# An attention norm with one activation in place of two, and the last tile's rows stored in six transfers in place of twelve

## The chip, the core and the metric

One Trainium2 chip, one of its cores. The metric is the device time of one execution in microseconds (us). The kernel before was timed three times: 264.51, 264.31 and 264.94 us, median 264.51. One more execution was taken with the hardware profiler; it took 264.59 us, and its span from the first to the last instruction is 262.6 us.

## The reference

Eight batches, eight heads, 576 positions, head size 64. Per head a 64 x 64 product of k and v, then q times it, then a norm over the 64 elements of each row; the heads are laid side by side into a token matrix of 4608 x 512, which goes through a two-layer network with a quick GELU.

```python
kv  = einsum('bhsd,bhse->bhde', k, v)
out = einsum('bhsd,bhde->bhse', q, kv)
rms = sqrt(mean(out * out, axis=-1) + 1e-6)
x   = (out / rms * g_norm) laid out as (4608, 512)
h   = x @ w_in                      # 512 -> 2048
g   = h * sigmoid(1.702 * h)
out = g @ w_out                     # 2048 -> 512, float32
```

## The kernel before

**Tiles.** The 4608 tokens are worked through in nine tiles of 512. Tile t (0 to 7) holds the first 512 positions of batch t. The 64 positions that each batch has left over are gathered in `x_rem` and make tile 8, which the code calls `t == B`. Batches 0 and 1 (`EARLY`) take their positions in another order, so that their left-over rows lie six rows apart in the output, where those of the other batches lie one below the other.

**Order.** The order of the instructions on each engine is the order in which the program issues them (`manual_schedule`). While the projections of tile t run on TensorE, the attention of batch t + 1 is slipped between them: `at1` and `at2` (lines 953 to 957) attach such units to the number of a matmul group, and the tables `FIRST`, `LATER` and `LAST_TWO` (lines 906 to 938) hold the numbers. Tiles 2 to 8 do their two matrix products by seven block products in place of eight (classes `SevenIn` and `Seven`).

**The norm.** There are two forms of it. Where the head elements lie along the partitions (batches 0 and 1, and the left-over 64 rows of every batch), `out` (line 260) makes the product, ScalarE squares it (line 272), a matmul with a block matrix of ones adds the squares up (`sums`, line 335), ScalarE takes the logarithm of the mean plus 1e-6 (line 337) and then `rs` (line 343) the exponential of minus half of that; VectorE multiplies (`apply`, lines 348 to 359). Where the rows lie along the partitions (the 512 rows of batches 2 to 7), VectorE adds the squares up (`add_up`), `roots` does the logarithm and the exponential on 128 x 16 elements, two times per batch (lines 310 and 311), and `turn` multiplies and has SP transpose the result by DMA. Logarithm and exponential come from one activation table set, the GELU from another; `preload_act_table_set` (lines 173, 331, 1005, 1019) loads them.

For batch 0 `sums` and `rs` are placed apart by hand (lines 857 to 871), with work for other heads in between; everywhere else `ss` calls one right after the other.

**The last tile's stores.** Tile 8 has 512 rows in four row blocks `mo` of 128 rows; block `mo` holds the left-over rows of batches 2 mo and 2 mo + 1, 64 partitions each. `Seven.run` (line 648) takes the block products of tile 8 in the order `LAST`; after the sums of a quarter `place` (line 629) puts them into `osb` on VectorE and calls `store_rest` (line 681): after the second quarter for blocks 0 and 1 with all 512 columns, then for block 2 and block 3 with the upper 256 columns, then for block 2 and block 3 with the lower 256. `store_rest` issues one transfer per batch: the first on SP's queue, the second on ScalarE's:

```python
for g in range(2):
    rows = out[(2 * mo + g) * S : (2 * mo + g + 1) * S, n0:n1]
    ...
    queue = (nc.sync, nc.scalar)[g]
    queue.dma_start(out=rows, in_=osb[g * R : (g + 1) * R, mo, n0:n1])
```

On the side of SBUF such a transfer counts 64 partitions, and on the side of DRAM 64 rows. The only other transfer on ScalarE's queue is that of `g_row` (line 136), 64 float32 in a single row.

Of the kernel before, what the change touches and what calls it, by code (L numbers as in the profile page):

```python
# [8 lines left out]
F32 = mybir.dt.float32  # L9
ALU = mybir.AluOpType  # L10
AFT = mybir.ActivationFunctionType

P = 128
# [3 lines left out]
def kernel(  # L17
# [10 lines left out]
    nc = tc.nc  # L28

    B, H, S, D = q.shape  # L30
    DM = H * D
# [5 lines left out]
    SM = 512  # L37
    J = SM // P
    R = S - SM
    assert R == 64 and B * R == SM and KO == NPAIR and 2 * D == P  # L40
    NT = B + 1
    EARLY = 2
    PE_ = 96
    NJ = S // PE_
# [5 lines left out]
    attn = ctx.enter_context(tc.tile_pool(name="attn", bufs=4))  # L50
# [20 lines left out]
    eps_t = const.tile([P, 1], F32)  # L71
# [4 lines left out]
    HF, HN = FO // 2, DM // 2  # L76
# [51 lines left out]
    for n in "kqv":  # L128
        if n != "q":
            rows = stage.tile([P, 6, 2 * P], F32, name="qf", tag="qf", bufs=2)  # L130
            rows = rows.rearrange("p h x -> p (h x)")[0:PE_]
# [8 lines left out]
        out=ident,  # L140
        in_=ident,
# [28 lines left out]
    load_w_in(10, 13)  # L170
    load_w_in(13, FO)

    nc.scalar.preload_act_table_set("natural_log_exp_and_others")
    nc.vector.memset(eps_t, EPS)
    one_t = const.tile([1, 1], F32)
    nc.vector.memset(one_t, 1.0)
# [18 lines left out]
    class Attention:  # L195
# [76 lines left out]
            nc.scalar.activation(sq[:, 0:n], t, AFT.Square)  # L272
            self.o[c] = (t, sq, n)

        def ss(self, c, table=False):
            self.sums(c, table)
            self.rs(c)


        def rows(self, i):  # L280

            pool, tag = (ps_h, "hT") if i < 3 else (ps_a, "att")
# [24 lines left out]

        def roots(self, h):
            s4 = self.sum4[:, 2 * h : 2 * h + 2, :]
            nc.scalar.activation(s4, s4, AFT.Ln, bias=eps_t, scale=1.0 / D)  # L310
            nc.scalar.activation(s4, s4, AFT.Exp, bias=0.0, scale=-0.5)

        def turn(self, j):
            j0, c0 = j // 2 * 2, j % 2 * (DM // 2)
# [11 lines left out]
                    in_=self.x16[:, j - 1 : j + 1, :].rearrange("p j n -> p (j n)"),  # L326
                )

        def sums(self, c, table=False):
            if table:  # L330
                nc.scalar.preload_act_table_set("natural_log_exp_and_others")
            o, sq, n = self.o[c]
            pool, tag = self.ss_pool
            t = pool.tile([P, SM], F32, name="ss", tag=tag)
            nc.tensor.matmul(t[:, 0:n], ones2, sq[:, 0:n], start=True, stop=True)  # L335
            ln = attn.tile([P, SM], F32, name="ln", tag="ln", bufs=2)
            nc.scalar.activation(ln[:, 0:n], t[:, 0:n], AFT.Ln, bias=eps_t, scale=1.0 / D)  # L337
            self.o[c] = (o, ln, n)

        def rs(self, c):  # L340
            o, ln, n = self.o[c]
            rs = attn.tile([P, SM], F32, name="rs", tag="rs", bufs=2)
            nc.scalar.activation(rs[:, 0:n], ln[:, 0:n], AFT.Exp, bias=0.0, scale=-0.5)
            self.o[c] = (o, rs, n)

        def apply(self, c):
# [142 lines left out]
    def copy(engine, to, src):  # L489
        (nc.vector.tensor_copy if engine == "D" else nc.scalar.copy)(to, src)  # L490
# [77 lines left out]
    class Seven:  # L568
# [60 lines left out]
        def place(self, name, mo, with_, i, j):  # L629
            ps, m = self.ready(name, mo)  # L630
            if ps is None:
                return
            o = osbs[self.t][:, 2 * i + m.start : 2 * i + m.stop, j * HN : (j + 1) * HN]
            if with_:
                nc.vector.tensor_add(o, ps, self.kept[with_][:, m])  # L635
            else:
                copy = nc.vector.tensor_copy if self.t == B else nc.scalar.copy
                copy(o, ps)  # L638
            if self.t == B:
                if (i, j) == (0, 1):  # L640
                    store_rest(0, 0, DM)
                    store_rest(1, 0, DM)
                elif i == 1:
                    store_rest(2 + mo, j * HN, (j + 1) * HN)
            elif self.t in HALVED and j == 1 - i:
                store(self.t, 2 * i, 2 * i + 2)

# [30 lines left out]
                            u()  # L678
                        n += 1

    def store_rest(mo, n0, n1):
        osb = osbs[B]
        for g in range(2):
            rows = out[(2 * mo + g) * S : (2 * mo + g + 1) * S, n0:n1]
            if 2 * mo + g < EARLY:
                p0 = SM % PE_
                rows = rows[bass.DynSlice(NJ * p0 + SM // PE_, R, step=NJ), :]
            else:
                rows = rows[SM:S, :]
            queue = (nc.sync, nc.scalar)[g]  # L690
            queue.dma_start(out=rows, in_=osb[g * R : (g + 1) * R, mo, n0:n1])

    def hid_seven(t, hid, seven, units1):

# [118 lines left out]
    def store(t, j0, j1):  # L813
        nc.sync.dma_start(
            out=out[t * S : t * S + SM, :].rearrange("(p j) m -> p j m", j=J)[:, j0:j1],
            in_=osbs[t][:, j0:j1],
        )


    a0 = First(0)  # L820
# [33 lines left out]
    a0.out(0)  # L854
    a0.q(1)
    a0.kv(1)
    a0.sums(0)
    a0.out(1)
    a0.q(2)
    a0.rs(0)  # L860
    a0.kv(2)
    a0.sums(1)
    a0.apply(0)
    a0.out(2)
    a0.rs(1)
    a0.q(3)
    a0.apply(1)
    d0 = Hidden(0)
    d0.mm(0, 0)
    a0.sums(2)  # L870
    a0.rs(2)
    d0.mm(0, 1)
    d0.mm(0, 2)
    d0.mm(0, 3, ps_a, "att")
# [29 lines left out]
    osbs = {}  # L904
# [35 lines left out]
    def plan(t):  # L940
        return LATER if t < B - 1 else LAST_TWO
# [7 lines left out]
    for t in range(NT):  # L949
        b = t + 1  # L950
        u1, u2 = {}, {}

        def at1(i, f, *args):
            u1.setdefault(i, []).append(lambda: f(*args))

        def at2(i, f, *args):
            u2.setdefault(i, []).append(lambda: f(*args))  # L957

        def of(b, name, *args):
            return lambda: getattr(live[b], name)(*args)  # L960

        if t == 0:
            at1(7, of(0, "out", NPAIR))
            at2(4, setattr, a0, "ss_pool", Attention.ss_pool)
            at2(4, of(0, "ss", NPAIR, True))
            at2(4, of(0, "apply", NPAIR))
            at1(8, start, 1)
            at2(5, scale_w_in, 0, nc.scalar)
            at2(6, scale_w_in, 1, nc.scalar)
            at2(33, weight_sum, 0)  # L970
            at2(33, scale_w_in, 2, nc.vector)
            at2(34, scale_w_in, 3, nc.vector)
            for n, at in ((2, 35), (0, 39), (1, 40)):
                at2(at, w_in_sum, n)
            for l in range(2):
                at1(9, nc.vector.memset, kvd[l], 0.0)
            at1(13, load_q, 2)
            for c in range(NPAIR):
                at1(12, of(1, "pack_q", c))
                at2(9 + 3 * c, of(1, "q", c))  # L980
                at2((36, 37, 46, 47)[c], of(1, "kv", c))
                o = (41, 43, 52, 53)[c]
                at2(o, of(1, "out", c))
                if c == NPAIR - 1:
                    at2(48, load_kv, 2)
                at2((45, 48, 56, 58)[c], of(1, "ss", c))
                at2((48, 51, 56, 60)[c], of(1, "apply", c))
        elif b < B:
            if t == 1:
                for n in range(1, 4):  # L990
                    at1(0, weight_sum, n)
                at1(9, w_in_sum, 3)
            todo = plan(t) if t >= SEVEN else None
            at1(todo.steps.index("kv") if todo else 11, of(b, "kv_all", todo.keep if todo else "D"))
            late = 15 if todo else 11
            if t == 1:
                at1(5, start, b)
                at1(5, of(b, "transpose_q"))
            if t + 2 < B:
                at1(late, load_kv, t + 2)  # L1000
                at1(late, load_q, t + 2)
                at2(100, start, t + 2)
                at2(100, of(t + 2, "transpose_q"))
            at = todo.attn if todo else FIRST
            at2(at["table"], nc.scalar.preload_act_table_set, "natural_log_exp_and_others")
            for h in range(2):
                at2(at["roots"][h], of(b, "roots", h))
            for j in range(J):
                for name in ("rows", "add_up", "turn"):
                    at2(at[name][j], of(b, name, j))  # L1010
            at2(46, of(b, "out", NPAIR))
            at2(74, of(b, "ss", NPAIR))
            at2(80, of(b, "apply", NPAIR))
            at2(82, nc.scalar.preload_act_table_set, "gelu_apprx_sigmoid_and_others")
        elif t < B:
            for name in ("ss_pool", "rest_pool"):
                at2(16, setattr, live[1], name, (ps_a, "att"))
            at2(16, of(1, "out", NPAIR))
            at2(34, nc.scalar.preload_act_table_set, "natural_log_exp_and_others")
            at2(44, of(1, "ss", NPAIR))  # L1020
            at2(50, of(1, "apply", NPAIR))
            at2(52, nc.scalar.preload_act_table_set, "gelu_apprx_sigmoid_and_others")
        dense(t, u1, u2, (GROUP, 5)[t] if t < 2 else 0, t == 0, None if t else d0)
# [30 lines left out]
```

## Time and profile before

| | |
|---|---|
| time, median of 3 | 264.51 us (264.31 to 264.94) |
| profiled execution | 264.59 us |
| its span, first to last instruction | 262.6 us |
| mean granted TensorE clock | 0.997 |
| TensorE matmul busy | 254.4 us, 97% of the span |
| VectorE busy | 185.6 us, 71% |
| ScalarE busy | 183.5 us, 70% |
| moved by DMA | 35.32 MB |

Times in the views count from the start of the span. PE is TensorE's matmuls, PEld its weight loads, DVE is VectorE, ACT is ScalarE, POOL is GpSimd, SP is SyncE; SPq and ACTq are the instructions with which SP and ScalarE issue transfers. A group of instructions reads: line, engine, operation, output<-input, shapes, count, then busy us, mean ns of one, idle us before them and what ended the idle time. A row of the busy view by stretches reads: the stretch and its length, the busy us (and count) of PE, PEld, DVE, ACT and POOL, the granted clock in that stretch, the busy share of the core's 16 DMA engines and the GB/s that they moved. A row of a DMA queue reads: packets, MB, and the time that the packets took as a share of 16 engines over the stretch asked for. q10 is ScalarE's DMA queue, q1 is SP's. The line on DMA packets counts those under 512 B, under 2 KB and under 8 KB, each number holding the one before it.

### The profile page before, as it was taken

To read this page: it belongs to the slowest core of one execution; us is meant where nothing else is said; L and a number is where in the kernel's file an instruction comes from. 1 tells how busy PE (TensorE), PEld (TensorE's weight loads), DVE (VectorE), ACT (ScalarE), POOL (GpSimd) and SP (SyncE) were. 2 spreads that over 40 slices of the span, in tenths; PEclk is the share of its full clock that TensorE was granted. 3 is DMA by queue.
4 is the path that set the end of the run, shared out by engine and by line. 5 is a ranking of instruction groups with operands and counts; after the bars stand their busy time and mean duration, and the time that the engine had idled before them with its cause. 6 is when DMAs were issued, how large, how long until landed. Compare 5 with 4: busy or idle time off the path is not lost.

```text
span 262.6 us, 6224 instructions
## 1 busy us (share of the span) xinstructions
PE 254.4 (97%) x2556; PEld 204.6 (78%) x2556; DVE 185.6 (71%) x324; ACT 183.5 (70%) x336; POOL 42.7 (16%) x66
## 2 busy tenths in 40 slices
PE   7789999999999999999999999999999999999993
PEld 6334444446988988899889988998899888888882
DVE  2540287768758995899589958995899677557841
ACT  3569856886648974897479847984699469837810
POOL 8864242005005000500050005000000000000000
PEclk9999999999999999999999999999999999999998
DMA  7999999998999946996799769946800620012005
GB/s 178 177 199 205 204 203 182 200 228 113 175 158 169 230 59 163 115 239 81 159 150 197 88 164 149 236 52 160 165 11 2 159 83 0 2 80 82 0 2 160
DMA packets 59870, 35.32 MB, mean 135 GB/s; under 512 B 31554, under 2 KB 57154, under 8 KB 59714
## 3 DMA queue, kind: packets, MB, share of 16 engines
q0 software_dynamic: 28512, 17.91, 49.7%
q1 hardware_dynamic: 30848, 16.49, 27.9%
q10 hardware_dynamic: 482, 0.52, 0.6%
q8 instruction: 20, 0.33, 0.5%
q14 instruction: 8, 0.07, 0.1%
HBM read 36.70 MB, written 9.44 MB: 176 GB/s over the span
## 4 chain that ended last, share of the span: by engine, by line
PE 93%; POOL 3%; DMA 3%; DVE 0%; issue 0%
PE o L658 37%; PE h L540 33%; PE hT L432 10%; PE o L770 5%; DMA vbuf<-in_v_dram 3%; PE kvp L221 2%; PE outR L286 2%; POOL qraw L89 1%; PE ss L335 1%; POOL kraw L89 1%; PE outT L254 0%; POOL vbuf L89 0%; PE q L413 0%; PE outT L258 0%; POOL w_in_sb L153 0%; DVE osb L638 0%
## 5 line engine op out<-in xcount | busy, mean ns | idle before, releaser
L658 PEld LDWEIGHTS <-gS 128*128 128x128 f16 x512 | 49.8, 98 | 5.6
L520 ACT ACTIVATE gT<-h 128x512 f16<-128x512 f32 x84 | 46.2, 605 | 5.2 <-PE h L540 5.2
L540 PEld LDWEIGHTS <-ws 128*128 128x128 f16 x448 | 43.8, 98 | 5.1
L658 PE MATMUL o<-tw,gS 128*128 128x256 f16 x384 | 46.3, 273 | 0.0
L540 PE MATMUL h<-xS,ws 128*128 128x256 f16 x336 | 45.3, 273 | 0.0
L658 PEld LDWEIGHTS <-gT 128*128 128x128 f16 x384 | 37.1, 98 | 4.2
L540 PEld LDWEIGHTS <-w_in_sb 128*128 128x128 f16 x336 | 32.5, 98 | 3.9
L658 PE MATMUL o<-w_out_sb,gT 128*128 128x256 f16 x256 | 33.3, 273 | 0.0
L432 PE MATMUL hT<-xT,w_in_sb 128*128 128x512 f16 x128 | 28.9, 379 | 0.7 <-DMA w_in_sb<-in_moe_w_in_dram 0.7
L540 PE MATMUL h<-xT,w_in_sb 128*128 128x256 f16 x192 | 27.1, 273 | 0.0
L635 DVE TENSOR_TENSOR osb<-o,qf 128x512 f32<-128x512 f32 (+1 forms) x25 | 16.7, 668 | 13.7 <-PE o L658 10.9
L89 POOL DMA_DIRECT2D kraw<-in_k_dram x11 | 8.0, 731 | 106.5 <-PE kvp L221 88.4
L554 DVE TENSOR_TENSOR h<-h,s 128x512 f32<-128x512 f32 x28 | 19.6, 698 | 7.4 <-PE h L540 5.6
L590 DVE TENSOR_TENSOR gS<-gT 128x512 f16<-128x512 f16 (+2 forms) x34 | 22.0, 653 | 3.9 <-ACT gT L441 3.2
L432 PEld LDWEIGHTS <-w_in_sb 128*128 128x128 f16 x128 | 12.3, 98 | 15.7 <-DMA w_in_sb<-in_moe_w_in_dram 1.3
L556 DVE TENSOR_TENSOR s<-h,s 128x512 f32<-128x512 f32 x28 | 19.4, 692 | 3.9 <-PE h L540 3.3
L441 ACT ACTIVATE gT<-hT 128x512 f16<-128x512 f32 x32 | 17.6, 613 | 5.4 <-PE hT L432 5.3
L337 ACT ACTIVATE ln<-ss,eps_t 128x512 f32<-128x512 f32 (+1 forms) x16 | 9.3, 581 | 14.0 <-PE ss L335 13.9
L520 ACT ACTIVATE gT<-s 128x512 f16<-128x512 f32 x28 | 17.3, 628 | 1.2 <-DVE s L556 1.2
L957 ACT ACT_TABLE_LOAD x14 | 18.0, 1283 | 0.2
L770 PE MATMUL o<-w_out_sb,gT 128*128 128x512 f16 x64 | 16.7, 380 | 0.0
L490 ACT COPY s<-h 128x512 f32<-128x512 f32 x17 | 10.0, 588 | 9.5 <-PE h L540 8.8
(94 smaller groups left out, 369.4 us busy)
## 6 DMA issues: line engine op xcount, KB each, us to landing
out_dram<-osb SPq DMA_DIRECT2D x10, 512.0 KB, 4.2
kraw<-in_k_dram POOLq DMA_DIRECT2D x6, 576.0 KB, 8.7
vbuf<-in_v_dram POOLq DMA_DIRECT2D x6, 576.0 KB, 12.2
qraw<-in_q_dram POOLq DMA_DIRECT2D x3, 512.0 KB, 13.2
qbuf<-in_q_dram POOLq DMA_DIRECT2D x3, 512.0 KB, 14.3
out_dram<-osb SPq DMA_DIRECT2D x6, 192.0 KB, 6.6
w_in_sb<-in_moe_w_in_dram POOLq DMA_DIRECT2D x4, 256.0 KB, 8.0
w_out_sb<-in_moe_w_out_dram POOLq DMA_DIRECT2D x2, 512.0 KB, 13.8
```

The lines of the kernel that those rows point to most:

```text
L89: nc.gpsimd.dma_start(out=raw[n][0:PE_, c0:c1, :].rearrange("p c (l x) -> p (c l) x", l=2), in_=early_src(n, b, c0, c1),)
L432: nc.tensor.matmul(self.h[fo], w_in_sb[:, ko, fo * P : (fo + 1) * P], self.x[:, ko], start=(ko == 0), stop=(ko == KO - 1),)
L441: nc.scalar.activation(self.gT[:, fo, :], self.h[fo], AFT.Gelu_apprx_sigmoid)
L520: nc.scalar.activation(self.gT[:, to, n * TH : (n + 1) * TH], src, AFT.Gelu_apprx_sigmoid)
L540: nc.tensor.matmul(bank[name][:, a], w, x, start=(p in (1, 5) and a == 0 and k == 0), stop=(k == KH - 1), skip_group_check=True,)
L554: nc.vector.tensor_add(bank["z"], bank["x"], self.s5)
L556: nc.vector.tensor_add(self.s5, bank["x"], self.s5)
L590: op(s[:, n, lo], a, b)
L635: nc.vector.tensor_add(o, ps, self.kept[with_][:, m])
L658: nc.tensor.matmul(o, a, w, start=(p in (1, 2, 5) and i == 0 and (mo == 0 or split)), stop=(i == HF - 1), skip_group_check=True,)
L770: nc.tensor.matmul(os[mo], gT[:, fo, mo * P : (mo + 1) * P], w_out_sb[:, fo, :], start=(fo == 0), stop=(fo == FO - 1),)
L957: u2.setdefault(i, []).append(lambda: f(*args))
```

## The change

It has two parts.

The norm: in `ss` (which takes in `sums` and `rs`) and in `roots` one activation, `Abs_reciprocal_sqrt`, with the same scale and the same bias operand takes the place of the logarithm and the exponential. The table set that is loaded for it is another one. For batch 0 the new activation stands where the logarithm stood; the places where the exponential stood are empty. `rs` has three buffers in place of two, the two `ln` buffers are gone.

The stores: `store_rest` issues one transfer for a row block and column range, both batches together. On the side of SBUF it counts 128 partitions; on the side of DRAM it counts 2 batches, 64 rows in each, one run of columns in each row. Blocks 0 and 2 and blocks 1 and 3 go by different queues, as the call says.

```diff
         def roots(self, h):
             s4 = self.sum4[:, 2 * h : 2 * h + 2, :]
-            nc.scalar.activation(s4, s4, AFT.Ln, bias=eps_t, scale=1.0 / D)
-            nc.scalar.activation(s4, s4, AFT.Exp, bias=0.0, scale=-0.5)
+            nc.scalar.activation(s4, s4, AFT.Abs_reciprocal_sqrt, bias=eps_t, scale=1.0 / D)
...
-        def sums(self, c, table=False):
+        def ss(self, c, table=False):
             if table:
-                nc.scalar.preload_act_table_set("natural_log_exp_and_others")
+                nc.scalar.preload_act_table_set("abs_reciprocal_sqrt_and_small")
             o, sq, n = self.o[c]
             pool, tag = self.ss_pool
             t = pool.tile([P, SM], F32, name="ss", tag=tag)
             nc.tensor.matmul(t[:, 0:n], ones2, sq[:, 0:n], start=True, stop=True)
-            ln = attn.tile([P, SM], F32, name="ln", tag="ln", bufs=2)
-            nc.scalar.activation(ln[:, 0:n], t[:, 0:n], AFT.Ln, bias=eps_t, scale=1.0 / D)
-            self.o[c] = (o, ln, n)
-
-        def rs(self, c):
-            o, ln, n = self.o[c]
-            rs = attn.tile([P, SM], F32, name="rs", tag="rs", bufs=2)
-            nc.scalar.activation(rs[:, 0:n], ln[:, 0:n], AFT.Exp, bias=0.0, scale=-0.5)
+            rs = attn.tile([P, SM], F32, name="rs", tag="rs", bufs=3)
+            nc.scalar.activation(
+                rs[:, 0:n], t[:, 0:n], AFT.Abs_reciprocal_sqrt, bias=eps_t, scale=1.0 / D
+            )
             self.o[c] = (o, rs, n)
...
                 if (i, j) == (0, 1):
-                    store_rest(0, 0, DM)
-                    store_rest(1, 0, DM)
+                    store_rest(0, 0, DM, nc.sync)
+                    store_rest(1, 0, DM, nc.scalar)
                 elif i == 1:
-                    store_rest(2 + mo, j * HN, (j + 1) * HN)
+                    store_rest(2 + mo, j * HN, (j + 1) * HN, (nc.scalar, nc.sync)[mo])
...
-    def store_rest(mo, n0, n1):
-        osb = osbs[B]
-        for g in range(2):
-            rows = out[(2 * mo + g) * S : (2 * mo + g + 1) * S, n0:n1]
-            if 2 * mo + g < EARLY:
-                p0 = SM % PE_
-                rows = rows[bass.DynSlice(NJ * p0 + SM // PE_, R, step=NJ), :]
-            else:
-                rows = rows[SM:S, :]
-            queue = (nc.sync, nc.scalar)[g]
-            queue.dma_start(out=rows, in_=osb[g * R : (g + 1) * R, mo, n0:n1])
+    def store_rest(mo, n0, n1, queue):
+
+        osb = osbs[B][:, mo, n0:n1]
+        rows = out.rearrange("(b s) m -> b s m", s=S)[2 * mo : 2 * mo + 2, :, n0:n1]
+        if 2 * mo < EARLY:
+            p0 = SM % PE_
+            rows = rows[:, bass.DynSlice(NJ * p0 + SM // PE_, R, step=NJ), :]
+        else:
+            rows = rows[:, SM:S, :]
+        queue.dma_start(out=rows, in_=osb)
...
     a0.q(1)
     a0.kv(1)
-    a0.sums(0)
+    a0.ss(0)
     a0.out(1)
     a0.q(2)
-    a0.rs(0)
     a0.kv(2)
-    a0.sums(1)
+    a0.ss(1)
     a0.apply(0)
     a0.out(2)
-    a0.rs(1)
     a0.q(3)
...
-    a0.sums(2)
-    a0.rs(2)
+    a0.ss(2)
```

The three other `preload_act_table_set` calls name the new set in the same way.

More of the change, by code (lines that the diff above doesn't have):

```diff
@@ L273, in out @@
             self.o[c] = (t, sq, n)
-        def ss(self, c, table=False):
-            self.sums(c, table)
-            self.rs(c)
         def rows(self, i):
@@ L327, in turn @@
                 )
-        def sums(self, c, table=False):
+        def ss(self, c, table=False):
             if table:
-                nc.scalar.preload_act_table_set("natural_log_exp_and_others")
+                nc.scalar.preload_act_table_set("abs_reciprocal_sqrt_and_small")
             o, sq, n = self.o[c]
@@ L1004 @@
             at = todo.attn if todo else FIRST
-            at2(at["table"], nc.scalar.preload_act_table_set, "natural_log_exp_and_others")
+            at2(at["table"], nc.scalar.preload_act_table_set, "abs_reciprocal_sqrt_and_small")
             for h in range(2):
@@ L1018 @@
             at2(16, of(1, "out", NPAIR))
-            at2(34, nc.scalar.preload_act_table_set, "natural_log_exp_and_others")
+            at2(34, nc.scalar.preload_act_table_set, "abs_reciprocal_sqrt_and_small")
             at2(44, of(1, "ss", NPAIR))
```

## The prediction

> **What bounds the kernel now.** I began with the page: the busy time by engine, and the chain that ended last.
>
> ```profile
> PE 254.4 (97%) x2556; PEld 204.6 (78%) x2556; DVE 185.6 (71%) x324; ACT 183.5 (70%) x336; POOL 42.7 (16%) x66
> ...
> PE 93%; POOL 3%; DMA 3%; DVE 0%; issue 0%
> ```
>
> TensorE is busy 97% of the span and is 93% of the chain. ScalarE, whose work the norm changes, is busy 70% and is not in the chain at all. So the next question is what TensorE ever waits for. The view of waits, asked for TensorE alone, answers with five lines, and this is all of it:
>
> ```profile
> PE idle L841 <- DVE one_t L176: 1.3, 1, 1.3
> PE kv L221 <- DMA vbuf<-in_v_dram: 0.9, 2, 0.6
> PE hT L432 <- DMA w_in_sb<-in_moe_w_in_dram: 0.7, 1, 0.7
> PE outT L254 <- DVE kvb L383: 0.4, 1, 0.4
> PE q L393 <- DMA qraw<-in_q_dram: 0.2, 1, 0.2
> ```
>
> The columns are us in total, times, longest. None of the five names ScalarE, and all lie in the start, where inputs arrive. Then the busy view by stretches:
>
> ```profile
> 16.60:31.00 14.40, 14.40 (x70) 6.48 (x70) 2.77 (x6) 12.26 (x21) 5.70 (x9) 1.00 1.32 203
> ...
> 233.60:258.10 24.50, 24.49 (x225) 21.71 (x222) 15.54 (x26) 13.67 (x27) 0.00 (x0) 1.00 0.17 62
> 258.10:262.60 4.50, 0.00 (x0) 0.00 (x0) 0.42 (x1) 0.00 (x0) 0.00 (x0) 0.83 0.46 138
> ```
>
> From 16.6 to 258.1 us TensorE is full. The last 4.5 us belong to no engine: one VectorE copy of 0.42 us, then only DMA. That tail is where the second part of the change works.
>
> **The norm.** The groups of ScalarE's instructions, shapes kept apart:
>
> ```profile
> L337 ACT ACTIVATE ln<-ss,eps_t 128x512 f32<-128x512 f32 x8 | 5.5, 689 | 2.5 <-PE ss L335 2.4
> L343 ACT ACTIVATE rs<-ln 128x512 f32<-128x512 f32 x8 | 5.0, 629 | 0.2
> ...
> L343 ACT ACTIVATE rs<-ln 128x256 f32<-128x256 f32 x8 | 3.3, 416 | 0.3
> ...
> L311 ACT ACTIVATE sum<-sum 128x16 f32<-128x16 f32 x12 | 2.6, 216 | 0.4
> ```
>
> The new function is in no row. It is bounded by 629 ns (an activation of that shape without a bias operand) and by 689 + 629 = 1318 ns (the two that it replaces); I take 689 ns, the logarithm's, because input, output and bias are the same. Then what goes is every exponential: 5.0 + 3.3 + 2.6 = 10.9 us of ScalarE's busy time. At the upper bound nothing goes, so the part can't cost.
>
> What hides it: TensorE, full beside all of it. The one place where the norm's latency comes close to TensorE is the last head pair of batch 0, in the timeline:
>
> ```profile
> 16.80 5.73 PE L432 MATMUL hT<-xT,w_in_sb 128*128 128x512 f16 x25
> ...
> 18.38 0.75 DVE L349 SCALAR_TENSOR_TENSOR xT<-outT,g_col,rs 128x512 f16<-128x512 f32 x1 [2.27 <-ACT rs L343]
> ```
>
> `xT` is whole at 18.38 + 0.75 = 19.13 us. In TensorE's order 11 matmuls stand before the first that reads it (one more for row 1, four for row 2, six for two further columns); 5.73 / 25 = 0.23 us each, so it is wanted at 16.80 + 11 x 0.23 = 19.3 us. It is in time, and there is no stall to remove; the change makes it about 0.6 us earlier, and what is late next is TensorE itself. If that cover were gone the chain could win those 0.6 us at most. The batch 0 activations that stood between heads have VectorE steps behind them that wait for TensorE or DMA as before. In the later tiles SP's transposes of `turn` start earlier, by the 0.2 to 0.4 us of the small exponentials; they wait for nothing that the change delays, and it is VectorE that reads their result, not TensorE. The table loads stay as many and stand in the same places. **Sum of the norm: 0**, with at most a few tenths of a us either way.
>
> **The stores.** Before, twelve transfers; in the view of line 691:
>
> ```profile
> L691 SPq DMA_DIRECT2D out_dram<-osb x6: 506/550/583, 255.4 to 258.6; - x6
> L691 ACTq DMA_DIRECT2D out_dram<-osb x6: 473/554/835, 255.4 to 259.3; - x6
> L691 ACTq EVENT_SEMAPHORE  x5: 17/17/17, 251.1 to 259.3; - x5
> ```
>
> Each issue takes about 0.55 us, six on each queue. The last copy ends at 258.1 + 0.42 = 258.55; SP issues its half at once (258.6), ScalarE only at 259.3, behind a semaphore wait. The change removes six issues and that wait; three are left on each queue, and nothing is queued behind them but the end of the program. That is the gain, if a transfer is as fast as before. Whether it is depends on how many DMA engines one transfer uses. The DMA view from 254 to 262.6 us:
>
> ```profile
> DMA packets 960, 1.05 MB, mean 122 GB/s; under 512 B 192, under 2 KB 704, under 8 KB 960
> ...
> q1 hardware_dynamic: 480, 0.52, 21.6%
> q10 hardware_dynamic: 480, 0.52, 19.2%
> ```
>
> 960 packets: 960 - 704 = 256 rows of 2 KB, 704 - 192 = 512 rows of 1 KB, and 192 small ones. 192 / 12 = 16 per transfer: one completion from each of 16 engines. Now the first 2 us, where ScalarE's queue carries only `g_row`, whose outermost count is 1 row:
>
> ```profile
> q10 hardware_dynamic: 2, 0.00, 0.1%
> ```
>
> Two packets: 256 bytes of data and **one** completion. So on these queues the count of engines is not fixed at 16; it went with the outermost count, 16 for 64 rows and 1 for 1 row. The new transfer counts 64 rows inside 2 batches on the DRAM side: its outermost count is 2. It can't be merged, because the batches do not lie one behind the other. My forecast is that it runs on **two engines**, one batch each.
>
> The Trainium skill, "DMA: Bandwidth & Descriptors", section "Why a DMA increments its semaphore by 16 and not by 1", states this as a rule: the transfer takes the largest number of engines up to 16 that divides the outermost counts of both sides; for 128 and 2 that is 2. By that rule the sum is the one below, and the two counts above (16 and 1) agree with it. The same page's "Rules for kernel authors" speaks for the change as well: it advises one 128-partition transfer in place of two over the halves, which is the first rival.
>
> What two engines cost. Prices of one packet on one engine, from DMA answers over three stretches: 8 KB rows (the store of tile 7; a slice reads 437 GB/s), 2 KB rows (257.25 to 257.5), 1 KB rows (259.0 to 259.25).
>
> ```profile
> GB/s 0 0 0 0 0 0 0 0 0 0 0 0 0 0 0 0 0 437 437 437 437 437 437 437 437 0 0 0 0 0 55 0 0 0 0 0 0 0 0 0
> ```
>
> ```profile
> q10 hardware_dynamic: 42, 0.09, 89.0%
> ```
>
> ```profile
> DMA packets 97, 0.08 MB, mean 332 GB/s; under 512 B 16, under 2 KB 97, under 8 KB 97
> ...
> q10 hardware_dynamic: 54, 0.05, 55.4%
> q1 hardware_dynamic: 43, 0.04, 45.2%
> ```
>
> - 2 KB: 0.890 x 16 x 0.25 us / 42 = 84.8 ns.
> - 1 KB: (0.554 + 0.452) x 16 x 0.25 us = 4.02 us for 81 rows and 16 completions. The two packets of `g_row` took 0.1% of 16 x 2 us, some 16 ns each; with about 0.2 us taken off for the completions, 3.82 / 81 = 47.2 ns.
> - Each of the two engines carries half: 128 x 84.8 + 256 x 47.2 ns = 10.9 + 12.1 = **22.9 us** (before rounding).
> - Lower bound: 437 / 16 = 27.3 GB/s per engine at 8 KB; 0.524 MB each gives 19.2 us. Upper bound: all packets of the tail took (21.6 + 19.2)% x 16 x 8.6 us = 56.1 us with both queues crowding each engine; half is 28.0 us.
>
> When it starts and ends:
>
> ```profile
> 256.50:257.00 0.50, 0.50 (x7) 0.45 (x5) 0.30 (x1) 0.00 (x0) 0.00 (x0) 1.00 0.84 176
> ...
> 260.50:261.00 0.50, 0.00 (x0) 0.00 (x0) 0.00 (x0) 0.00 (x0) 0.00 (x0) 1.00 0.51 123
> 261.00:261.50 0.50, 0.00 (x0) 0.00 (x0) 0.00 (x0) 0.00 (x0) 0.00 (x0) 0.56 0.00 0
> ```
>
> Data begins at 256.5 us, 1.1 after the first issue; it ends at 261.0, and 1.6 us more pass to the end of the span. The first two transfers alone (0.52 MB) keep two engines until 256.5 + 10.9 = 267.4, long after the last is issued, so the engines never run dry: 256.5 + 22.9 + 1.6 = 281.0 us of span. The profiled execution took 264.59 us, 2.0 more than its span, and 0.1 more than the median run. **Forecast: 281.0 + 2.0 = 283.0 us**, 18.4 more than before (7%). Its bounds: 256.5 + 19.2 + 3.6 = 279.3 and 256.5 + 28.0 + 3.6 = 288.1; 0.5 on either side for the norm and for the waits at the end gives 278.8 to 288.6.
>
> **The rivals.**
>
> 1. *Faster: all 16 engines carry the new transfers*, split by the 128 partitions of the other side. For it: nothing in the trace shows a transfer whose two sides count differently. Against it: `g_row`'s single completion. Its time: SP issues its third and last at 258.6 unhindered, data follows 1.1 us later at 259.7, 128 rows of 47.2 ns on 16 engines are 0.4 us; data ends at 260.1 to 260.2 in place of 261.0, so 264.59 - 0.8 = 263.8 us, 0.3% faster. The point that decides: the data must end by 261.0, 4.5 us after it starts; 2 x 22.9 = 45.8 engine-us / 4.5 needs more than 10 engines. With 8 it is already slower.
> 2. *Slower, but a little: two engines per transfer, each time another pair*, so that six transfers share twelve engines. The last is issued at 258.6, data from 259.7, 64 rows of 1 KB on one engine are 3.0 us: 262.7, so 264.59 + 1.7 = 266.3 us. The trace shows no pair being chosen, so neither for nor against.
> 3. *The norm does not do what it says*: if the new table set lacks the square, ScalarE loads tables back and forth between squares and roots. Against it: before, squares run right behind the GELU and right behind the logarithm's set, without a load. A load takes 1.28 us:
>
> ```profile
> L957 ACT ACT_TABLE_LOAD x14 | 18.0, 1283 | 0.2
> ```
>
>    From 41 to 49 us ScalarE goes from squares to roots and back some three times for batch 1: 6 x 1.28 = 7.7 us, less the four exponentials that go (2.5 us), up to 5 us more, on top of any case: 283 to 288 us with the first.
>
> **How the numbers follow.** Two engines 0.82 (283.0 us), 16 engines 0.12 (263.8 us), other pairs 0.05 (266.3 us), one engine or something else 0.01; the third rival, 0.03, lies across them. The range of the first case holds nearly all of its 0.82, so 278.8 to 288.6 us leaves no more than 2 in 10 out. About 0.2% is what a measurement of this kernel can tell from no change. Faster by more than that is rival 1, less a quarter of it for a smaller gain: 0.09; within 0.2%: 0.03; slower: 0.88.
>
> **What would show it.** In the profile after, the DMA view of the tail should have 6 x 2 = 12 completions in place of 192, the same 768 rows, a busy share near 2/16 = 0.125 for over 20 us, some 46 GB/s, and no engine busy after 258.6 us. The first store's time to landing should go from 3 us to 11. The chain should end in DMA of `osb`. For the norm: no logarithm or exponential rows, the new rows near 689, 474 and 306 ns, ScalarE's busy time down by 10.9 us, TensorE's waits after 16.6 us as empty as before, and the last copy again at 258.1. What would make me wrong: 96 completions, and the last landing near 260.5 us.

## The result, and the profile after

The changed kernel takes 282.2 us (median of 6, 281.83 to 282.87) against 264.42 us for the kernel before on the same chip: a ratio of 1.0655, 95% interval 1.0617 to 1.0694. The forecast was 283.0. The profiled execution took 282.22 us, 1.8 more than its span. From the page of the changed kernel:

```profile
span 280.4 us, 6199 instructions
...
PE 254.4 (91%) x2556; PEld 204.7 (73%) x2556; DVE 185.2 (66%) x324; ACT 173.6 (62%) x308; POOL 42.5 (15%) x66
```

TensorE is busy for the same 254.4 us as before; only its share fell, because the span grew by 17.8 us, from 262.6 to 280.4. The view of `osb` from 250 us on shows that the computation ends no later (the last copy starts at 257.8, before at 258.1), and has the issues of the six new transfers. The columns are shortest, median and longest ns, then first and last start:

```profile
L680 SPq DMA_DIRECT2D out_dram<-osb x3: 522/633/5102, 255.1 to 258.3; - x3
L680 ACTq DMA_DIRECT2D out_dram<-osb x3: 632/795/8676, 255.1 to 257.4; - x3
L628 DVE COPY osb<-o x2: 425/425/425, 256.9 to 257.8; 128x256 f32<-128x256 f32 x2
```

The DMA view from 254 us to the end answers the question on which the forecast hung. A slice of its GB/s line is 0.66 us:

```profile
GB/s 0 0 0 19 19 25 25 37 50 53 50 53 50 53 50 53 50 53 48 51 51 50 47 50 48 48 48 48 50 47 50 47 50 48 48 48 48 29 0 0
DMA packets 780, 1.05 MB, mean 40 GB/s; under 512 B 12, under 2 KB 524, under 8 KB 780
...
q1 hardware_dynamic: 390, 0.52, 6.0%
q10 hardware_dynamic: 390, 0.52, 5.3%
```

The rows are the same 768 (780 - 12), but the small packets went from 192 to 12: two completions for each of six transfers in place of sixteen for each of twelve. The busy view by stretches shows the share that belongs to it, and where it starts and ends:

```profile
256.00:256.50 0.50, 0.50 (x7) 0.45 (x5) 0.42 (x1) 0.00 (x0) 0.00 (x0) 1.00 0.07 16
...
259.50:260.00 0.50, 0.00 (x0) 0.00 (x0) 0.00 (x0) 0.00 (x0) 0.00 (x0) 1.00 0.14 53
260.00:266.00 6.00, 0.00 (x0) 0.00 (x0) 0.00 (x0) 0.00 (x0) 0.00 (x0) 0.65 0.13 51
266.00:272.00 6.00, 0.00 (x0) 0.00 (x0) 0.00 (x0) 0.00 (x0) 0.00 (x0) 0.50 0.13 49
272.00:278.00 6.00, 0.00 (x0) 0.00 (x0) 0.00 (x0) 0.00 (x0) 0.00 (x0) 0.50 0.14 48
278.00:279.00 1.00, 0.00 (x0) 0.00 (x0) 0.00 (x0) 0.00 (x0) 0.00 (x0) 0.50 0.11 40
279.00:280.40 1.40, 0.00 (x0) 0.00 (x0) 0.00 (x0) 0.00 (x0) 0.00 (x0) 0.50 0.00 0
```

The next to last column is the share of 16 engines: 0.13 to 0.14, close to 2/16 = 0.125, for some 19 us in which no engine of the core computes. The column before it falls to 0.50 only there: the mean clock of 0.967 of this profile belongs to TensorE's idle tail and explains nothing. The waits of SP name the same thing (us in total, times, longest):

```profile
SPq L1035 <- DMA out_dram<-osb: 15.6, 3, 7.7
```

The norm did what it says too. ScalarE's groups have no logarithm and no exponential any more:

```profile
L331 ACT ACTIVATE rs<-ss,eps_t 128x512 f32<-128x512 f32 x8 | 5.4, 694 | 2.9 <-PE ss L329 2.9
...
L331 ACT ACTIVATE rs<-ss,eps_t 128x256 f32<-128x256 f32 x8 | 3.8, 474 | 13.5 <-PE ss L329 13.5
L305 ACT ACTIVATE sum<-sum,eps_t 128x16 f32<-128x16 f32 x12 | 3.6, 307 | 0.1
```

694, 474 and 307 ns, within 5 ns of the logarithm's durations; ScalarE is busy 9.9 us less (183.5 to 173.6), with 28 instructions fewer and as many table loads as before (18), so the third rival is out. The forecast was 10.9 us less; the exponentials had run partly beside their neighbours (in the timeline before, one from 44.55 to 45.18 us and the next square from 45.09), and the busy time counts such stretches once.

### The profile page after: what moved, and what is told of

It reads as the page before. It is cut to its first block, busy times and chain, and to the rows that moved or that the text cites. A ratio compares the mean times of both kernels' runs of the same rounds, so it can differ in the third digit from the quotient of the medians.

```text
span 280.4 us, 6199 instructions
## 1 busy us (share of the span) xinstructions
PE 254.4 (91%) x2556; PEld 204.7 (73%) x2556; DVE 185.2 (66%) x324; ACT 173.6 (62%) x308; POOL 42.5 (15%) x66
## 4 chain that ended last, share of the span: by engine, by line
PE 86%; POOL 2%; DMA 2%; DVE 0%; issue 0%; ACT 0%; ACTq 0%
PE o L648 35%; PE h L530 31%; PE hT L422 9%; PE o L759 5%; PE kvp L221 2%; DMA vbuf<-in_v_dram 2%; PE outR L281 2%; POOL qraw L89 1%; PE ss L329 1%; POOL kraw L89 1%; PE outT L254 0%; POOL vbuf L89 0%; PE q L403 0%; PE outT L258 0%; ACT sq L272 0%
## 5 line engine op out<-in xcount | busy, mean ns | idle before, releaser
L331 ACT ACTIVATE rs<-ss,eps_t 128x512 f32<-128x512 f32 (+1 forms) x16 | 9.2, 584 | 16.4 <-PE ss L329 16.4
L296 DVE TENSOR_REDUCE sum<-sq 128x8 f32<-128x512 f16 x24 | 15.9, 680 | 0.9 <-ACT sq L290 0.6
```

Source lines behind the costliest of these rows:

```text
L296: nc.vector.tensor_reduce(out=self.sum4[:, j, :], in_=self.o[j][1].rearrange("p (x d) -> p x d", d=D), op=ALU.add, axis=mybir.AxisListType.X,)
```

## The experiments

Theory: the engines of a transfer follow the outermost count of its pattern, the two engines make the whole loss, and the norm is beside it. The rivals: a transfer over 128 partitions, or one whose sides count differently, is slow in itself; merging two transfers into one is what costs; the norm has a part in it. Each ratio is to the kernel before, timed on the same chip as the run.

**The parts apart.** First the new norm with the old stores, then the old norm with the new stores.

```diff
+            nc.scalar.activation(
+                rs[:, 0:n], t[:, 0:n], AFT.Abs_reciprocal_sqrt, bias=eps_t, scale=1.0 / D
+            )
...
     def store_rest(mo, n0, n1):
         osb = osbs[B]
         for g in range(2):
```

> The kernel before with the new norm alone; the twelve stores stay as they were. Theory (the norm lies beside a full TensorE, the stores make all of the loss): 264.2 us, 0.0 to 0.4 us below the kernel before, with ScalarE's busy time near 173.6 us. Rival 1 (the norm costs something that the stores hid): above 264.6 us. Rival 2 (the exponentials were on the path): below 263.5 us.

Measured: 263.9 us, ratio 0.9973 (0.9954 to 0.9991), ScalarE busy 173.5 us. A small gain, so rival 1 is out; rival 2's bound, below 263.5 us, is not reached.

```diff
-            queue = (nc.sync, nc.scalar)[g]
-            queue.dma_start(out=rows, in_=osb[g * R : (g + 1) * R, mo, n0:n1])
...
+        osb = osbs[B][:, mo, n0:n1]
+        rows = out.rearrange("(b s) m -> b s m", s=S)[2 * mo : 2 * mo + 2, :, n0:n1]
...
+        queue.dma_start(out=rows, in_=osb)
```

> The kernel before with the new stores alone, the logarithm and the exponential kept. Theory: 282.4 us, the whole of the loss, with 12 completions and two engines. Rival (the two parts add to each other): under 280 us.

Measured: 282.31 us, ratio 1.0661 (1.0615 to 1.0708), the whole loss. Its DMA view of the tail repeats the one above:

```profile
DMA packets 780, 1.05 MB, mean 40 GB/s; under 512 B 12, under 2 KB 524, under 8 KB 780
```

**The same six transfers with another outermost count.** The rows of the two batches are put on the partitions in turn, where VectorE writes `x_rem`, so that the DRAM side can count the 64 rows first:

```diff
-                    x_rem[:, :, self.b * R : (self.b + 1) * R],
+                    x_rem[:, :, self.b // 2 * P : (self.b // 2 + 1) * P].rearrange(
+                        "p c (r g) -> p c r g", g=2
+                    )[:, :, :, self.b % 2],
...
-        queue.dma_start(out=rows, in_=osb)
+        queue.dma_start(out=rows.rearrange("b s m -> s b m"), in_=osb)
```

> The changed kernel with one thing turned: the left-over rows of two batches lie in turn on the partitions (row 0 of the even batch, row 0 of the odd one, row 1 ...), so that the same six transfers count 64 rows x 2 batches on the DRAM side, outermost 64, in place of 2 x 64. Theory (the engines of a transfer follow the outermost count): 16 completions per transfer, 96 in all, data ends near 260.1 us, about 263.8 us in all, 0.6 us below the kernel before. Rival (a transfer whose two sides count differently, or which takes 128 partitions at once, is slow in itself): near 282 us, as the changed kernel.

Measured: 263.23 us, ratio to the kernel before 0.9951 (0.9926 to 0.9976), 19 us below the changed kernel. The DMA view from 254 us and the issues:

```profile
GB/s 0 0 0 0 0 0 0 0 0 0 0 0 0 237 388 410 377 345 377 399 324 340 340 340 270 313 329 43 0 140 356 194 0 0 0 0 0 0 0 0
DMA packets 864, 1.05 MB, mean 138 GB/s; under 512 B 96, under 2 KB 608, under 8 KB 864
```

```profile
L682 SPq DMA_DIRECT2D out_dram<-osb x3: 539/550/627, 255.2 to 258.4; - x3
L682 ACTq DMA_DIRECT2D out_dram<-osb x3: 546/651/852, 255.2 to 257.5; - x3
```

96 completions, sixteen each, mostly at over 300 GB/s in place of 50. These transfers also take 128 partitions, also merge two batches, and their sides also count differently (128 against 64 x 2). The rival that such a transfer is slow in itself falls with this run.

**The same version with the old norm:**

> The kernel before with the six transfers over rows that lie in turn on the partitions, and the old norm. Theory (stores and norm add up, each measured alone): the tail gains 0.7 to 0.8 us, the norm's 0.2 us is missing, 263.6 us. Rival (the gain of the version with both came from the norm alone): 264.4 us.

Measured: 263.4 us, ratio 0.9954 (0.9926 to 0.9983). The last copy in the view of `osb`, and the span:

```profile
L640 DVE COPY osb<-o x2: 425/425/425, 256.8 to 257.7; 128x256 f32<-128x256 f32 x2
```

```profile
span 261.3 us, 6213 instructions
```

The gain of the store survives without the norm, so the rival falls. The intervals of this run and of the one with both overlap, so they can't show how much the norm adds to it.

**Twelve transfers, other outermost counts.** The stores of the kernel before, one batch each, with the DRAM side cut in two. A first try wrote 4 blocks of 16 rows:

```diff
+            rows = rows.rearrange("(a r) m -> a r m", a=4)
```

> The kernel before with its twelve stores of 64 rows, whose DRAM side is written as 4 blocks of 16 rows: same rows, same count of transfers, same queues, outermost count 4. Theory: 4 engines per transfer, 48 completions, 45.8 engine-us / 4 = 11.4 us of data, so 256.5 + 11.4 + 1.6 + 2.0 = 271.5 us. Rival (the loss comes from the merging of two transfers into one, not from the outermost count): 264.5 us, as the kernel before. If the library folds the 4 and the 16 back into 64, it is also 264.5 us, with 192 completions, and tells nothing.

Measured: 264.24 us, ratio 1.0007 (0.9976 to 1.0037), and 192 completions:

```profile
DMA packets 960, 1.05 MB, mean 122 GB/s; under 512 B 192, under 2 KB 704, under 8 KB 960
```

Sixteen completions each, the third case that was foreseen: the two counts went out as one of 64, so the run tells nothing of a count of 4. The next three take the rows in turn, so that the counts can't be folded; the left-over rows of a batch then come out in another order, and these versions serve for their times alone:

```diff
+            rows = rows.rearrange("(r a) m -> a r m", a=2)
```

> The kernel before with its twelve stores, each of one batch and 64 rows, but the rows are written as 2 outer times 32 inner ones, row 2r + a for partition 32a + r, so that the two counts can't be folded into one; the left-over rows of a batch come out in another order. Outermost count 2. Theory (engines follow the outermost count): 24 completions, two engines, 45.6 engine-us / 2 = 22.8 us of data, 282.3 us. Rival (the merging of two batches into one transfer is what costs): 264.4 us with 192 completions.

> As the run before, with 4 outer times 16 inner rows. Theory: 48 completions, 45.6 / 4 = 11.4 us of data, 256.5 + 11.4 + 1.6 + 2.0 = 271.5 us. Rival (only a count of 2 goes wrong): 264.4 us.

> As the run before, with 8 outer times 8 inner rows. Theory: 96 completions, 45.6 / 8 = 5.7 us of data, 256.5 + 5.7 + 1.6 + 2.0 = 265.8 us. Rival: 264.4 us.

Their DMA views from 254 us, in this order; a slice is 0.68, 0.43 and 0.28 us:

```profile
GB/s 0 0 0 21 9 33 27 36 39 42 33 48 54 48 54 48 54 48 53 50 50 50 51 48 48 48 48 48 48 48 50 47 48 50 48 48 48 17 0 0
DMA packets 792, 1.05 MB, mean 38 GB/s; under 512 B 24, under 2 KB 536, under 8 KB 792
```

```profile
GB/s 0 0 0 0 0 53 10 19 53 77 62 81 101 86 96 77 67 57 72 86 103 96 96 96 98 98 96 93 98 93 96 98 93 93 55 46 7 0 0 0
DMA packets 816, 1.05 MB, mean 61 GB/s; under 512 B 48, under 2 KB 560, under 8 KB 816
```

```profile
GB/s 0 0 0 0 0 0 0 0 0 0 52 96 52 81 170 177 207 192 207 188 170 166 185 192 181 181 185 192 192 181 177 185 151 22 0 0 0 0 0 0
DMA packets 864, 1.05 MB, mean 95 GB/s; under 512 B 96, under 2 KB 608, under 8 KB 864
```

| outermost count | completions per transfer | GB/s once running | expected us | measured us | ratio (95%) |
|---|---|---|---|---|---|
| 2 | 24 / 12 = 2 | 48 | 282.3 | 283.41 | 1.0694 (1.0602 to 1.0785) |
| 4 | 48 / 12 = 4 | 96 | 271.5 | 273.19 | 1.0308 (1.022 to 1.0396) |
| 8 | 96 / 12 = 8 | 185 | 265.8 | 266.8 | 1.0075 (1.0041 to 1.0109) |
| 64 (before) | 192 / 12 = 16 | about 300 | | 264.42 | |

Completions and rate follow the count step by step, with no transfer merged. So the rival of the merging falls as well, and so does the one by which only a count of 2 goes wrong. All three are 1.0 to 1.7 us above the expectation. One reason is on show: the sum let the data run at full rate from the first moment, and the lines above begin with some 5.5, 3.0 and 1.1 us below it.

## Why the prediction was right

**The bound.** TensorE full from 16.6 us on and a tail that only DMA fills: the profile after has the same 254.4 us of TensorE and a longer tail.

**Two engines.** Shown by the completions, by the share of 0.13, and by the three runs with other counts. What was read off two counts (16 and 1) holds at 2, 4 and 8. The share also decides against the second rival, another pair of engines for each transfer: both queues move data at once, and together they keep about two engines busy. Which of the two carries which batch, no view shows. The rule of the Trainium skill, "DMA: Bandwidth & Descriptors", section "Why a DMA increments its semaphore by 16 and not by 1", gives the same numbers, and these runs agree with it at every step. The section counts the slowest dimension that is not of size 1, where the prediction wrote outermost; for the stores here the two are the same, and the 64 elements in the single row of `g_row` did not count as such a dimension, as its one completion shows. The same page's advice under "Rules for kernel authors" to move two halves by one 128-partition transfer held here with an outermost count of 64 (263.23 us) and not with one of 2 (282.2 us).

**The price.** 22.9 us of data were forecast and 22.6 measured, from 256.3 to 278.9. The busy view in quarters of a microsecond has the two ends; the stretch before the first and the one behind the last have a share of 0.00:

```profile
256.25:256.50 0.25, 0.25 (x4) 0.23 (x3) 0.23 (x1) 0.00 (x0) 0.00 (x0) 1.00 0.14 33
...
278.75:279.00 0.25, 0.00 (x0) 0.00 (x0) 0.00 (x0) 0.00 (x0) 0.00 (x0) 0.50 0.04 12
```

That it came so close is luck in part. The prices of a packet held. The queues from 262 to 266 us, where all rows have 2 KB, and from 274 to 278 us, where all have 1 KB (two of the 190 packets are completions):

```profile
q1 hardware_dynamic: 50, 0.10, 6.6%
q10 hardware_dynamic: 50, 0.10, 6.6%
...
q1 hardware_dynamic: 95, 0.10, 6.8%
q10 hardware_dynamic: 95, 0.10, 6.7%
```

13.2% x 16 x 4 us / 100 = 84.5 ns, and 13.5% x 16 x 4 us / 190 = 45.5 ns (forecast 84.8 and 47.2). What the sum had wrong is that it set these times end to end: 13.2% and 13.5% are more than the 12.5% of two engines that work on one packet at a time, so the packets overlap a little. Once running, two engines moved 48 to 53 GB/s, some 24.5 each, more than the 22.9 that the sum comes to (0.524 MB in 22.9 us) and less than the bound of 27.3. Against that, the first 3.7 us carried 0.12 MB only (the eight half-us stretches from 256 to 260 run from 16 to 53 GB/s). Without that start, 1.05 MB at 49 GB/s would have taken 21.4 us. The two errors nearly cancel.

**The norm at 0.** Nearly right, but one step of it failed: "there is no stall to remove". There was one, of 0.13 us, and the view of TensorE's waits in the prediction can't show it, because it is booked on the weight load. In the timeline before, at the last sum of squares of batch 1:

```profile
45.22 0.69 DVE L353 TENSOR_TENSOR xT<-outT,rs 128x512 f16<-128x512 f32 x1 [0.60 <-ACT rs L343]
...
45.82 0.68 DVE L779 COPY osb<-o 128x512 f32<-128x512 f32 x1
46.01 0.59 PE L770 MATMUL o<-w_out_sb,gT 128*128 128x512 f16 x2
...
46.55 0.10 PEld L335 LDWEIGHTS <-ones 128*128 128x128 f16 x1 [0.45 <-DVE osb L779]
46.56 0.39 PE L335 MATMUL ss<-sq,ones 128*128 128x512 f16 x1
```

The exponential delays VectorE's multiplication, that delays the copy of `o`, and the matmul waits for the buffer that the copy empties (both are taken from the pool `ps_h` under the tag `hT`): two matmuls of 0.216 us from 46.01 end their turn at 46.44, the next starts at 46.56. After:

```profile
44.36 0.69 DVE L343 TENSOR_TENSOR xT<-outT,rs 128x512 f16<-128x512 f32 x1
...
44.97 0.68 DVE L768 COPY osb<-o 128x512 f32<-128x512 f32 x1
...
45.81 0.59 PE L759 MATMUL o<-w_out_sb,gT 128*128 128x512 f16 x2
...
46.24 0.38 PE L329 MATMUL ss<-sq,ones 128*128 128x512 f16 x1
```

45.81 + 0.43 = 46.24: no gap. From batch 1's first product of k and v to batch 2's it takes 19.70 to 19.71 us in all the profiles with the old norm and 19.57 in all with the new one. In the stretch before that, from batch 0's last sum of squares on, it takes 21.95 to 22.05 us with the old and 21.88 to 21.97 with the new. That difference is not the norm's: it is one gap on TensorE, of 0.02 to 0.18 us, where a weight load waits for the arrival of `w_in`. In the profile before:

```profile
18.04 0.33 PEld L432 LDWEIGHTS <-w_in_sb 128*128 128x128 f16 x3 [0.49 <-DMA w_in_sb<-in_moe_w_in_dram]
```

After batch 2's products no profile differs. Nor was the last head pair the one place where the norm comes close to TensorE. In the run with 4 blocks of 16 rows, which has the old norm, the first head pair of batch 0 was late for TensorE:

```profile
11.83 0.75 DVE L349 SCALAR_TENSOR_TENSOR xT<-outT,g_col,rs 128x512 f16<-128x512 f32 x1 [0.23 <-ACT rs L343]
...
12.63 0.38 PE L432 MATMUL hT<-xT,w_in_sb 128*128 128x512 f16 x1 [0.21 <-DVE xT L349]
```

TensorE waited 0.69 us for `v` two microseconds later, longer than those 0.21, so it would hardly have won by them.

So the traces show 0.13 us for the norm on TensorE. The interval of the first run, 0.9954 to 0.9991, is a gain of 0.2 to 1.2 us, and 0.13 lies just below it. What makes the rest stays open; the arrival of the inputs shifts the whole program by more than that from one execution to the next (batch 0's last sum of squares starts between 16.05 and 16.88 us in these ten profiles).

**Rival 1's sum** was right in size where its condition was given: 0.8 us were forecast for six transfers on 16 engines. In the run with the old norm the tail, from the start of the last copy to the end of the span, is 261.3 - 257.7 = 3.6 us, before 262.6 - 258.1 = 4.5. The gain is the wait and the six issues that the prediction named.

**Signs that did not show as announced.** The chain that ended last does not end in DMA: the view follows it back from the last copy (257.80 us) and leaves the tail out, so that its shares add up to some 90%. Nor does the page give the new transfers a time to landing; SP's waits, 15.6 us with a longest of 7.7, stand in for it. The completions tell more: the DMA view from 266.25 to 266.75 us has the first two packets under 512 B, so the first store landed 11.2 to 11.7 us after its issue at 255.1, where 11 were forecast.

**The remaining 0.8 us** between 283.0 and 282.2: data begins 0.2 us earlier (256.3 in place of 256.5) and takes 0.3 less (22.6 in place of 22.9), 1.5 us in place of 1.6 pass from its end to the end of the span, and 1.8 in place of 2.0 lie outside it.

## What to carry to other kernels

Merge two stores into one only if the merged pattern still counts its rows first: write both sides down, look at the outermost count of each, and if a batch or a head stands there, turn the layout on the chip so that rows do. Here 64 rows first gave sixteen engines, and counts of 2, 4 and 8 gave as many engines as they say; no run tried other counts. In the DMA view, completions divided by transfers give the number of engines without any timing. And look for TensorE's waits among its weight loads too, not only among its matmuls.

## What the runs showed of the hardware that was not expected

The instruction that issues a transfer can itself be held for microseconds. With two engines the third issue on each queue took 8676 ns (ScalarE) and 5102 ns (SP), against some 550 ns in the run with 64 rows counted first. Here nothing stood behind them. In the middle of a kernel, work that stands behind such an issue on ScalarE would presumably wait; no run here shows it.

A transfer on few engines is slow to come to its rate: at two engines, 16 GB/s at first and 50 only after some 3 us, though the first transfer of each queue holds 128 rows. In that time only one of the two queues moved data, though both issued their first transfer at 255.1. The DMA view from 256 to 258.5 us has SP's queue and no other:

```profile
DMA packets 24, 0.05 MB, mean 20 GB/s; under 512 B 0, under 2 KB 0, under 8 KB 24
...
q1 hardware_dynamic: 24, 0.05, 11.0%
```

Its rows took 11.0% x 16 x 2.5 us / 24 = 183 ns each, against 84.5 ns later, when both queues run. What holds them back in that time is not settled.
